# A gated GELU layer on one core: unit 1's weights loaded ahead of the transposed rows, and its raw products computed ahead of unit 0's second half

## The chip, the cores and the metric

The kernel runs on one core of a Trainium2 chip. The metric is the device time of one execution in microseconds. Times of two kernels are compared between runs of the same rounds on the same chip. All runs here were fast, with a granted TensorE clock of 0.999 to 1.0.

Names in the profile: PE is TensorE's matmuls and PEld its weight loads; DVE is VectorE, ACT ScalarE, POOL GpSimd; SPq is the queue that issues the DMA loads. A "bank" is one of the eight PSUM tiles of 128 x 512 float32 values in which TensorE leaves its products.

## The reference

```python
B, S, Dm, Df = 1, 2048, 1024, 3584           # all bfloat16
g = einsum("bsd,df->bsf", x, w_gate)
u = einsum("bsd,df->bsf", x, w_up)
h = gelu(g) * u                              # tanh form
return einsum("bsf,fd->bsd", h, w_down)
```

## The kernel before

The kernel goes through the rows of x in two passes of 1024 rows, each as two chunks of 512 columns of x transposed, `xT[0]` and `xT[1]`. In a pass it goes through 14 "units", each of 256 columns of `w_gate` and `w_up`. A unit is made by a Strassen-like scheme: seven products in place of eight, with sums of weight blocks (`s1` to `s4`, `sa`) and of x blocks (`t1` to `t4`, `tb`) made by VectorE, ScalarE and GpSimd. "Raw" products take w and xT as they are. Later stages do the same for `w_down`.

The change touches the opening only. Unit 0 of the first pass is done plainly (`plain`), chunk by chunk, because the sums are not ready yet. Unit 1 is the first by the scheme. Engines run what is listed for them in program order, except where a wait holds them.

```python
# the sums of one unit's weights (sh is 128 x 512)
"s1": lambda q: [new(eng, a21[i], a22[i], ADD, "s1", sh) for i in GU],
"s2": lambda q: [new(eng, q["s1"][i], a11[i], SUB, "s2", sh) for i in GU],
"s3": lambda q, GU=GU: [new(eng, a11[i], a21[i], SUB, "s3", sh) for i in GU],
"s4": lambda q: [new(eng, a12[i], q["s2"][i], SUB, "s4", sh) for i in GU],
"sa": lambda q: [cast(a22[i], "sa", sh) for i in GU],        # ScalarE
# ... and of x: t1 = lo1 - lo0, t2 = hi1 - t1, t3 = hi1 - lo1, t4 = hi0 - t2 (VectorE), tb = cast(hi1)

def unit(u, banks, xT, w, s, t, p1, after_p5, aside, keep, ahead_of_p4, snap_first):
    e, c, d = banks                      # for unit 1: banks 0-1, 2-3, 4-5
    for i in GU: product(c[i], w[:, i, KH:, :P], b21, True)      # raw
    aside(-2)
    g, up = add(c, p1)                   # two VectorE sums
    aside(-1)
    for i in GU: product(e[i], s["s2"][i], t["t2"], False)
    aside(0)
    # ... (copies of e; then c = d, banks 4 and 5)
    for i in GU: product(c[i], s["s1"][i], t["t1"], True)
    # ...
    for i in GU: product(e[i], s["s3"][i], t["t3"], False)
    # ...
    for i in GU: product(c[i], s["s4"][i], t["tb"], False)
    # ... (then the next unit's first raw product, then sa x t4)

# the loads of the opening, all on one queue
xn0 = load_x(0)                                     # 512 plain rows, transposed on PE
for k0, k1 in ((0, 2), (2, 5), (5, NKB)):
    load_wf(nc.sync, k0, k1)                        # unit 0's weights
for ko in range(KH):
    transposing(xT, 1, ko, N)                       # rows 512-1023, blocks 0-3, transposing DMA
w = load_w(1)                                       # unit 1's weights, 1 MB
for ko in range(KH, NKB):
    transposing(xT, 1, ko, N)                       # blocks 4-7
ahead = load_w(2)

# the work of the opening
plain(bank[0:4], 0, range(0, 2), parts=2)           # unit 0, first half of the rows
plain(bank[0:4], 0, range(2, NKB))
t.make("t1")
finish(bank[0:4], 0)                                # gelu on ScalarE, hT = g * bank on VectorE
plain(bank[4:8], 1, range(KH))                      # unit 0, second half, blocks 0-3
s.make("s1", "s2")
nxt = {"p1": first_product(odd, xT, w)}             # unit 1, raw

def rest_of_0(part):                                # called by unit 1's aside(-2), aside(-1)
    if part == 0:
        t.make("t2", "tb")
        plain(bank[4:8], 1, range(KH, NKB))         # blocks 4-7
        pool_behind(t["t2"][-1])                    # GpSimd waits for the last t2
        s["s3"] = on_pool(s, range(1))              # s3 on GpSimd
    else:
        t3 = t["how"]["t3"](t, range(0, 2))
        pool_behind(t3[-1])
        s["s3"] += on_pool(s, range(1, 2))
        finish(bank[4:8], 1)
        t["t3"] = t3 + t["how"]["t3"](t, range(2, KH))
        s.make("sa")
# and aside(0) makes s4, then t4
```

`finish` reads bank 5 in a VectorE multiply, and unit 1's `s1·t1` product writes bank 5 soon after. PE cannot start it before that multiply has ended.

Of the kernel before, what the change touches and what calls it, by code (L numbers as in the profile page):

```python
# [10 lines left out]
def kernel(  # L11
# [32 lines left out]
    ADD, SUB, MUL = ALU.add, ALU.subtract, ALU.mult  # L44
# [6 lines left out]
    NKB = Dm // P  # L51
    KH = NKB // 2
    NFB = Df // P
    NJ = NFB // 2
    N = 512
# [20 lines left out]
    def new_x():  # L76
        return [xpool.tile([P, NKB, N], bf16, name=f"xT{c}") for c in range(2)]
# [4 lines left out]
    def slot(shape, dtype, name):  # L82
        return kpool.tile(shape, dtype, name=name, tag="k")


    bank = [psum.tile([P, N], f32, name=f"bank{i}") for i in range(8)]
    even, odd, cc, dd = bank[6:8], bank[0:2], bank[2:4], bank[4:6]
# [7 lines left out]
    def new(eng, a, b, op, name, shape=None, dtype=None):  # L95
        t = slot(shape or [P, N], dtype or f32r, name)
        eng(t, a, b, op)
        return t

    def cast(src, name, shape=None):  # L100
        t = slot(shape or [P, N], f32r, name)
        nc.scalar.copy(out=t, in_=src)  # L102
        return t

    def snap(ps, name):
        t = slot([P, N], f32, name)
        nc.scalar.copy(out=t, in_=ps)  # L107
        return t

    def matmul(ps, lhs, rhs, start, stop):  # L110
        nc.tensor.matmul(  # L111
            ps, lhsT=lhs, rhs=rhs, start=start, stop=stop, skip_group_check=True
        )
# [35 lines left out]
    def sums_s(w, eng):  # L149
        GU = range(2)  # L150
        sh = [P, KH, P]
        a11, a21 = [[w[:, i, :KH, h : h + P] for i in GU] for h in (0, P)]
        a12, a22 = [[w[:, i, KH:, h : h + P] for i in GU] for h in (0, P)]
        return Sums(
            how={
                "s1": lambda q: [new(eng, a21[i], a22[i], ADD, "s1", sh) for i in GU],
                "s2": lambda q: [new(eng, q["s1"][i], a11[i], SUB, "s2", sh) for i in GU],
                "s3": lambda q, GU=GU: [new(eng, a11[i], a21[i], SUB, "s3", sh) for i in GU],
                "s4": lambda q: [new(eng, a12[i], q["s2"][i], SUB, "s4", sh) for i in GU],
                "sa": lambda q: [cast(a22[i], "sa", sh) for i in GU],  # L160
            }
        )

    def pool_behind(tile):
        nc.gpsimd.tensor_copy(out=seen, in_=tile[:, :1].bitcast(f32))
# [19 lines left out]
    def product(ps, lhs, rhs, start):  # L185
        for k in range(KH):
            matmul(ps, lhs[:, k, :], rhs[k], start and k == 0, k == KH - 1)

    def first_product(e, xT, w):
        for i in range(2):  # L190
            product(e[i], w[:, i, :KH, :P], [xT[0][:, k, :] for k in range(KH)], True)
        return [snap(e[i], "p1") for i in range(2)]
# [160 lines left out]
    sa = {}  # L353
# [97 lines left out]
    def transposing(xT, c, ko, r0):  # L451
        nc.sync.dma_start_transpose(
            out=xT[c][:, ko, :], in_=x2[r0 : r0 + N, ko * P : (ko + 1) * P]
        )
# [12 lines left out]
    xT = new_x()  # L467
    xn0 = load_x(0)
    wf = wpool.tile([P, 2, NKB, 2 * P], bf16, name="w")
    for k0, k1 in ((0, 2), (2, 5), (5, NKB)):  # L470
        load_wf(nc.sync, k0, k1)
    for ko in range(KH):
        transposing(xT, 1, ko, N)
    w = load_w(1)
    for ko in range(KH, NKB):
        transposing(xT, 1, ko, N)
    ahead = load_w(2)

    def plain(ps, c, kos, parts=1):
        n = N // parts  # L480
        for k in range(kos.start, kos.stop, 2):
            for part in range(parts):
                cols = slice(part * n, (part + 1) * n)
                for p, (j, i) in zip(ps, [(j, i) for j in range(2) for i in range(2)]):
                    for ko in (k, k + 1):
                        matmul(
                            p[:, cols],
                            wf[:, i, ko, j * P : (j + 1) * P],
                            xT[c][:, ko, cols],
                            ko == 0 and part == 0,  # L490
                            ko == NKB - 1,
                        )

    def finish(ps, c):
        for j in range(2):
            times(j, c, gelu(ps[2 * j]), ps[2 * j + 1])

    on_dve, on_act = nc.vector.tensor_copy, nc.scalar.copy
    s, t = sums_s(w, dve), sums_t(xT)
    with tc.manual_schedule(engines={ENG.Activation}):  # L500
        def keep_warm(n, cols):
            for _ in range(n):
                nc.tensor.matmul(  # L503
                    bank[3][:, :cols], lhsT=warm[:, :P], rhs=warm[:, :cols], start=True, stop=True
                )

        keep_warm(NWARM, N)
        for i in range(NS):
            if i > 0:
                keep_warm(3, 2 * P)  # L510
            turn(xT, xn0, 0, i, on_act if i == 1 else on_dve)
        plain(bank[0:4], 0, range(0, 2), parts=2)
        plain(bank[0:4], 0, range(2, NKB))
        t.make("t1")
        finish(bank[0:4], 0)
        plain(bank[4:8], 1, range(KH))
        s.make("s1", "s2")
        nxt = {"p1": first_product(odd, xT, w)}

    seen = xpool.tile([P, 1], f32, name="seen")  # L520
    on_pool = sums_s(w, pool)["how"]["s3"]

    def rest_of_0(part):
        if part == 0:
            t.make("t2", "tb")
            plain(bank[4:8], 1, range(KH, NKB))
            pool_behind(t["t2"][-1])
            s["s3"] = on_pool(s, range(1))
        else:
            t3 = t["how"]["t3"](t, range(0, 2))  # L530
            pool_behind(t3[-1])
            s["s3"] += on_pool(s, range(1, 2))
            finish(bank[4:8], 1)
            t["t3"] = t3 + t["how"]["t3"](t, range(2, KH))
            s.make("sa")

    def making(u):
        if u < 2 or u >= NU:
# [3 lines left out]
    for ip in range(NPASS):  # L542
        for u in range(1 if ip == 0 else 0, NU):
            js = making(u) if ip == 0 else []

            def prepare():
                nonlocal ahead
                if first:
                    pool_behind(t["t4"][-1])
                nxt["w"], nxt["s"] = ahead, None  # L550
                if u + 1 < NU:
                    nxt["s"] = make_s(ahead, pool)
                if u + 2 < NU:
                    ahead = load_w(u + 2)
                if len(js) == 1:
                    store_made(js[0])
                for j in js[1:]:
                    keep_whole(j)
                if ip == 0:
                    fetch_wd(making(u + 1))  # L560

            def keep(part, ps):
                if js:
                    keep_part(js[0], part, ps)

            def aside(part):
                if (ip, u) == (0, 1) and part < 0:
                    rest_of_0(part + 2)
                if part == 0 and "s4" not in s:
                    s.make("s4")  # L570
                    t.make("t4")

            def ahead_of_p4():
                if u + 1 < NU:
                    nxt["p1"] = first_product(even if u % 2 else odd, xT, nxt["w"])

            e = odd if u % 2 else even
            p1 = nxt.pop("p1", None) or first_product(e, xT, w)
            first = (ip, u) == (0, 1)
            with tc.manual_schedule(engines={ENG.Activation}) if first else nullcontext():  # L580
                unit(u, (e, cc, dd), xT, w, s, t, p1, prepare, aside, keep, ahead_of_p4, first)
            if u + 1 < NU:
                w, s = nxt["w"], nxt["s"]

        last = ip == NPASS - 1
        got, nxt = {}, {}

        def more(step):

            nonlocal ahead  # L590
            if last:
                return
            if step in (-1, 0, 2):
                store_made({-1: NJ - 3, 0: NJ - 2, 2: NJ - 1}[step])
            if step == 0:
                xT[:] = new_x()
            if step >= 24 and step % 2 == 0 and step // 2 - 12 < len(moves):
                c, ko = moves[step // 2 - 12]
                transposing(xT, c, ko, (2 * (ip + 1) + c) * N)
            if step == 50:  # L600
                got["w"], ahead = load_w(0), load_w(1)
            if step == 58:
                got["s"] = make_s(got["w"], dve)
            if step == 62:
                got["t"] = make_t(xT)

        down(ip, even + cc, dd + odd, last, more)
        even, odd, cc, dd = odd, even, dd, cc
        if not last:
            w, t, s = got["w"], got["t"], got["s"]  # L610
# [29 lines left out]
```

## Time and profile before

| | before |
|---|---|
| time, median of 3 runs (542.34 to 542.64) | 542.6 us |
| profiled span | 540.5 us |
| PE busy | 533.0 us, 99% |
| first product of unit 0 | 7.48 us |
| first `s2·t2` product of unit 1 | 24.73 us |
| first `s4·tb` product of unit 1 | 30.39 us |

Before the change, the page's row of busy times (us, share of the span, instructions) and its summary of the chain that ended last read as follows.

```profile
PE 533.0 (99%) x2380; PEld 378.3 (70%) x2414; DVE 340.8 (63%) x524; ACT 258.3 (48%) x463; POOL 238.9 (44%) x217
...
PE 98%; DMA 1%; issue 0%; SPq 0%; ACT 0%
```

PE is the engine that decides. A busy share of 99% alone would not prove that nothing is lost. The Trainium skill ("Trainium Kernel Development and Optimization", Performance Expectations) warns that matmul busy time is a bad metric for how close a kernel is to roofline, because matmuls are pipelined, and here weight loads are busy only 70%. So the count of matmuls is better. In PE's timeline (start, duration, engine, line, operation, out<-in, shape and count; idle time before in brackets), the opening looks like this:

```profile
7.48 17.61 PE L111 MATMUL bank<-xT,w 128*128 128x256 bf16 x86
24.73 5.82 PE L111 MATMUL bank<-t,s 128*128 128x512 f32 x24
30.39 1.97 PE L111 MATMUL bank<-tb,s 128*128 128x512 f32 x8
```

From 7.48 to 24.73 us PE does the work of 80 full-size bf16 matmuls, 0.216 us each. (The program has 88 here, 16 of them half-size; a few records are missing from the x86.) The following 24 take 5.66 us to the start of `tb`. No row has idle time in brackets.

VectorE's timeline in the same stretch does have idle time, and the DMA queue's timeline tells why:

```profile
11.06 1.92 DVE L90 TENSOR_TENSOR t<-xT,xT 128x512 fp32r<-128x512 bf16 x3 [2.69 <-DMA xT<-in_x_dram]
15.10 0.69 DVE L90 TENSOR_TENSOR t<-xT,xT 128x512 fp32r<-128x512 bf16 x1 [2.12 <-DMA xT<-in_x_dram]
15.71 1.28 DVE L90 TENSOR_TENSOR hT<-g,bank 128x512 bf16<-128x512 f32 x2
...
18.67 0.69 DVE L90 TENSOR_TENSOR s<-w 128x512 fp32r<-128x512 bf16 x1 [1.05 <-DMA w<-in_w_up_dram]
...
20.49 2.49 DVE L90 TENSOR_TENSOR t<-xT,t 128x512 fp32r<-128x512 bf16 x4
...
24.09 1.40 DVE L90 TENSOR_TENSOR t<-xT 128x512 fp32r<-128x512 bf16 x2
25.41 1.27 DVE L90 TENSOR_TENSOR hT<-g,bank 128x512 bf16<-128x512 f32 x2
26.61 1.47 DVE L90 TENSOR_TENSOR t<-xT 128x512 fp32r<-128x512 bf16 x2
```

```profile
6.22 5.47 SPq L452 DMA_TRANSPOSE xT<-in_x_dram  x4
11.73 0.58 SPq L121 DMA_DIRECT2D w<-in_w_gate_dram  x1
12.36 0.58 SPq L121 DMA_DIRECT2D w<-in_w_up_dram  x1
12.98 6.71 SPq L452 DMA_TRANSPOSE xT<-in_x_dram  x4
```

VectorE loses 2.69 + 2.12 + 1.05 us waiting for loads, but PE does not notice. The operand `t2` ends at 22.98 us and PE wants it from 24.73. The second pair of hT multiplies (25.41) frees bank 5 at about 26.1 us, and PE gets to bank 5 at about 24.73 + 12 x 0.236 = 27.6 us. The last `t3` ends at 28.1 us, and PE wants it at 24.73 + 19 x 0.236 = 29.2 us.

### The profile page before, as it was taken

How to read it: one execution, taken by the hardware profiler on the slowest of the kernel's cores; microseconds unless marked ns; L12 is line 12 of the kernel's file. 1: busy time of each engine (PE TensorE's matmuls, PEld its weight loads, DVE VectorE, ACT ScalarE, POOL GpSimd, SP SyncE). 2: the span in 40 equal slices, each digit the busy share in tenths (PEclk: the TensorE clock that was granted, in tenths of full speed). 3: DMA queues.
4: the chain of work that ended last, by engine and by line, in shares of the span. 5: the costliest groups of instructions: out<-in, count | busy, mean ns of one | idle time of the engine just before them, and what ended most of it. 6: DMA issues, size and time to landing. Idle time of an engine off the chain costs nothing.

```text
span 540.5 us, 7403 instructions
## 1 busy us (share of the span) xinstructions
PE 533.0 (99%) x2380; PEld 378.3 (70%) x2414; DVE 340.8 (63%) x524; ACT 258.3 (48%) x463; POOL 238.9 (44%) x217
## 2 busy tenths in 40 slices
PE   8999999999999999999999999999999999999997
PEld 5577777667766746888876776677777775488885
DVE  3896666766666895684945545555544559676730
ACT  2566666566665410255355555555555541114431
POOL 0169966677774400000097777777766600000000
PEclk9999999999999999999999999999999999999999
DMA  8965666666655899969672222222331069473751
GB/s 198 201 185 177 175 183 203 191 183 200 201 165 172 269 382 329 285 180 301 224 194 79 78 79 78 79 79 79 85 100 49 2 200 369 150 235 96 227 192 49
DMA packets 108133, 93.28 MB, mean 173 GB/s; under 512 B 17216, under 2 KB 92992, under 8 KB 108096
## 3 DMA queue, kind: packets, MB, share of 16 engines
q1 hardware_dynamic: 108096, 92.82, 58.8%
q8 instruction: 19, 0.31, 0.3%
q14 instruction: 18, 0.15, 0.1%
HBM read 74.45 MB, written 15.20 MB: 166 GB/s over the span
## 4 chain that ended last, share of the span: by engine, by line
PE 98%; DMA 1%; issue 0%; SPq 0%; ACT 0%
PE bank L111 98%; DMA xn<-in_x_dram 1%; PE bank L448 0%; SPq L441 0%; ACT st L412 0%; PE bank L503 0%
## 5 line engine op out<-in xcount | busy, mean ns | idle before, releaser
L93 POOL TENSOR_TENSOR s<-w 128x512 fp32r<-128x512 bf16 x102 | 119.4, 1191 | 154.7 <-DVE t L90 87.6
L111 PE MATMUL bank<-t,s 128*128 128x512 f32 x648 | 157.0, 398 | 0.0
L111 PEld LDWEIGHTS bank<-t,s 128*128 128x128 f32 x648 | 121.7, 188 | 27.7
L107 ACT COPY p<-bank 128x512 f32<-128x512 f32 x124 | 70.4, 591 | 97.4 <-PE bank L111 97.4
L111 PE MATMUL bank<-xT,w 128*128 128x512 bf16 (+1 forms) x476 | 110.6, 376 | 1.9
L90 DVE TENSOR_TENSOR hT<-g,bank 128x512 bf16<-128x512 f32 x112 | 76.6, 686 | 53.2 <-ACT g L179 47.7
L111 PEld LDWEIGHTS <-w 128*128 128x128 bf16 x504 | 45.1, 98 | 59.1 <-issue 13.4
L90 DVE TENSOR_TENSOR sum<-bank,p 128x512 f32<-128x512 f32 x54 | 37.3, 692 | 53.0 <-PE bank L111 51.3
L179 ACT ACTIVATE g<-sum 128x512 f32<-128x512 f32 x81 | 51.4, 635 | 34.1 <-DVE sum L90 33.1
L111 PE MATMUL bank<-q 128*128 128x512 f32 x240 | 58.9, 389 | 0.0
L111 PE MATMUL bank<-t,sa 128*128 128x512 f32 x216 | 58.6, 413 | 0.0
L93 POOL TENSOR_TENSOR s<-w,s 128x512 fp32r<-128x512 bf16 x50 | 57.6, 1172 | 0.0
L93 POOL TENSOR_TENSOR s<-s,w 128x512 fp32r<-128x512 f32 x50 | 57.1, 1164 | 0.0
L111 PE MATMUL bank<-tb,s 128*128 128x512 f32 x216 | 53.3, 389 | 0.0
L111 PEld LDWEIGHTS bank<-q 128*128 128x128 f32 x240 | 45.0, 188 | 9.3
L111 PE MATMUL bank<-raw,hT 128*128 128x512 bf16 x218 | 48.4, 379 | 0.3
L111 PEld LDWEIGHTS bank<-t,sa 128*128 128x128 f32 x216 | 40.7, 188 | 10.6
L111 PEld LDWEIGHTS bank<-tb,s 128*128 128x128 f32 x216 | 40.5, 188 | 8.4
L102 ACT CAST tb<-raw 128x512 fp32r<-128x512 bf16 x28 | 17.2, 626 | 59.8 <-DMA raw<-in_w_down_dram 26.3
L107 ACT COPY u<-bank 128x512 f32<-128x512 f32 x62 | 35.9, 590 | 18.6 <-PE bank L111 18.6
L90 DVE TENSOR_TENSOR bank<-bank,p 128x512 f32<-128x512 f32 x54 | 37.8, 699 | 8.5 <-PE bank L111 5.2
L90 DVE TENSOR_TENSOR q<-hT 128x512 fp32r<-128x512 bf16 x56 | 38.4, 686 | 4.8 <-PE bank L111 4.8
(45 smaller groups left out, 442.6 us busy)
## 6 DMA issues: line engine op xcount, KB each, us to landing
raw<-in_w_down_dram SPq DMA_DIRECT2D x80, 256.0 KB, 4.7
q<-td SPq DMA_DIRECT2D x60, 256.0 KB, 4.9
w<-in_w_gate_dram SPq DMA_DIRECT2D x27, 512.0 KB, 5.2
w<-in_w_up_dram SPq DMA_DIRECT2D x27, 512.0 KB, 6.3
td<-m SPq DMA_DIRECT2D x12, 768.0 KB, 4.6
w<-td SPq DMA_DIRECT2D x6, 1024.0 KB, 10.1
out_dram<-st SPq DMA_DIRECT2D x32, 128.0 KB, 1.7
td<-w SPq DMA_DIRECT2D x2, 768.0 KB, 7.0
```

The lines of the kernel that those rows point to most:

```text
L90: nc.vector.tensor_tensor(out=out, in0=a, in1=b, op=op)
L93: nc.gpsimd.tensor_tensor(out=out, in0=a, in1=b, op=op)
L102: nc.scalar.copy(out=t, in_=src)
L107: nc.scalar.copy(out=t, in_=ps)
L111: nc.tensor.matmul(ps, lhsT=lhs, rhs=rhs, start=start, stop=stop, skip_group_check=True)
L179: nc.scalar.activation(g, src, ACT.Gelu_apprx_tanh)
```

## The change

What the edit does: plain loads are issued in one run and transposing loads in one run, and the work is ordered to fit. Unit 1's weights come first, so its raw products, which need only `xT[0]`, go ahead of all of unit 0's second half, which needs the late `xT[1]`. The sums of weights come ahead of the sums of x, and `s3` no longer needs GpSimd.

```diff
 # loads
-    for ko in range(KH):
-        transposing(xT, 1, ko, N)
     w = load_w(1)
-    for ko in range(KH, NKB):
+    for ko in range(NKB):
         transposing(xT, 1, ko, N)
 # work
         plain(bank[0:4], 0, range(2, NKB))
+        s["s1"] = s["how"]["s1"](s, range(1))
+        finish(bank[0:4], 0)
+        s["s1"] += s["how"]["s1"](s, range(1, 2))
+        nxt = {"p1": first_product(odd, xT, w)}
+        s.make("sa", "s2", "s3", "s4")
         t.make("t1")
-        finish(bank[0:4], 0)
-        plain(bank[4:8], 1, range(KH))
-        s.make("s1", "s2")
-        nxt = {"p1": first_product(odd, xT, w)}
 # rest_of_0
         if part == 0:
+            plain(bank[4:8], 1, range(NKB))
             t.make("t2", "tb")
-            plain(bank[4:8], 1, range(KH, NKB))
-            pool_behind(t["t2"][-1])
-            s["s3"] = on_pool(s, range(1))
         else:
             t3 = t["how"]["t3"](t, range(0, 2))
-            pool_behind(t3[-1])
-            s["s3"] += on_pool(s, range(1, 2))
             finish(bank[4:8], 1)
             t["t3"] = t3 + t["how"]["t3"](t, range(2, KH))
-            s.make("sa")
 # aside(0): s4 is no longer made here, only t4  (cut: the GU argument moves from s3 to s1,
 # and the line that defines on_pool goes)
```

More of the change, by code (lines that the diff above doesn't have):

```diff
@@ L155, in sums_s @@
             how={
-                "s1": lambda q: [new(eng, a21[i], a22[i], ADD, "s1", sh) for i in GU],
+                "s1": lambda q, GU=GU: [new(eng, a21[i], a22[i], ADD, "s1", sh) for i in GU],
                 "s2": lambda q: [new(eng, q["s1"][i], a11[i], SUB, "s2", sh) for i in GU],
-                "s3": lambda q, GU=GU: [new(eng, a11[i], a21[i], SUB, "s3", sh) for i in GU],
+                "s3": lambda q: [new(eng, a11[i], a21[i], SUB, "s3", sh) for i in GU],
                 "s4": lambda q: [new(eng, a12[i], q["s2"][i], SUB, "s4", sh) for i in GU],
@@ L513 @@
         plain(bank[0:4], 0, range(2, NKB))
+        s["s1"] = s["how"]["s1"](s, range(1))
[3 more added lines that the diff above has]
+        s.make("sa", "s2", "s3", "s4")
         t.make("t1")
-        finish(bank[0:4], 0)
-        plain(bank[4:8], 1, range(KH))
-        s.make("s1", "s2")
-        nxt = {"p1": first_product(odd, xT, w)}
     seen = xpool.tile([P, 1], f32, name="seen")
-    on_pool = sums_s(w, pool)["how"]["s3"]
     def rest_of_0(part):
         if part == 0:
+            plain(bank[4:8], 1, range(NKB))
             t.make("t2", "tb")
-            plain(bank[4:8], 1, range(KH, NKB))
-            pool_behind(t["t2"][-1])
-            s["s3"] = on_pool(s, range(1))
         else:
             t3 = t["how"]["t3"](t, range(0, 2))
-            pool_behind(t3[-1])
-            s["s3"] += on_pool(s, range(1, 2))
             finish(bank[4:8], 1)
             t["t3"] = t3 + t["how"]["t3"](t, range(2, KH))
-            s.make("sa")
     def making(u):
@@ L568, in aside @@
                     rest_of_0(part + 2)
-                if part == 0 and "s4" not in s:
-                    s.make("s4")
+                if part == 0 and "t4" not in t:
                     t.make("t4")
```

## The prediction

> **What bounds the kernel now.** TensorE. The page's busy row gives PE 533.0 of 540.5 us (99%); the chain that ended last is 98% matmuls, DMA 1%. PE waits for x rows and their transposes until 7.5 us. In the timeline the opening's products run from 7.48 to 24.73 us: 80 full-size matmuls in 17.25 us, 0.216 us each, and the only wait listed there is 0.26 us for weights. So there is no hole of a microsecond to win; the change can save almost nothing on PE and can only open a new hole.
>
> **What the change moves.** No matmul is added or removed. On PE, the 16 raw products of unit 1 (3.4 us) go ahead of all 32 of unit 0's second half (6.8 us). On the queue, unit 1's weights go ahead of all eight transposing loads. In the before trace they are issued at 11.73 and land at 18.67 us, and VectorE waits three times: 2.7 + 2.1 us for transposed rows, 1.1 us for weights. After, the weights should land near 11.5 and 13 us (1 MB behind the first weights at the 290 GB/s of the DMA view), transposed rows by about 20 us, ahead of PE's need (17.8 to 23 us). These waits go, but VectorE's work is reordered: all s sums first, t1 and t2 last, and the two s3 sums move from GpSimd (1.17 us each) to VectorE (0.62 us cadence, +1.2 us).
>
> **What that costs.** VectorE starts in earnest only when the first gelus end (13.47 and 14.33 us + 0.6). From the second hT multiply at 14.95 us: it, s1, 2 s2, 2 s3, 2 s4, 4 t1, 4 t2 are 16 operations at 0.615 us, so t2 ends at 24.9 us instead of 22.98. Two sums, two t3, then the multiply that frees the fourth unit-0 bank: it ends at 27.9 us instead of 26.1. PE reaches that bank (second half of s1·t1) at 24.73 + 12 x 0.236 = 27.6 us and waits about 0.4 us. The last t3 comes at 29.8 us; PE wants it at 29.7: another 0.1 to 0.2 us. The t2 operands just arrive in time. Total +0.6 us, never recovered, since later units are back to back on PE (12.60 us each). GpSimd has unit 2's s2 ready near 37.0, PE wants it near 37.9: no further wait.
>
> The Trainium skill ("SBUF — State Buffer", engine-port section) says that a GpSimd operation and a VectorE one with two SBUF inputs lock each other out. One t3 of before took 0.869 us against 0.68 beside GpSimd's s3; this goes, worth 0.2 us of VectorE at most.
>
> **Prediction:** 543.2 us, range 542.3 to 544.4. Faster by over 2%: 0.003; within 2%: 0.99; slower by over 2%: 0.007.
>
> **What would show it.** PE's s/t stage still starts at 24.6 to 24.8 us; little or no VectorE wait for transposed rows; VectorE gapless from 15 to 32 us; a PE wait of 0.3 to 0.6 us near 27.6 us on the hT multiply, a smaller one on t3; the tb product starts near 31.0 instead of 30.39 us; then a constant shift to the end.
>
> **What would make it wrong.** Weights landing after 14 us (each microsecond adds one to PE's wait). Transposes slower in one run of eight, so that t1 or PE wait: up to +2 us. VectorE faster without GpSimd: then the waits vanish, 542.5. A gain over 0.3 us would mean a hidden PE loss in the opening.

## The result

| | before | changed |
|---|---|---|
| time, median of 6 runs | 542.38 us (542.08 to 542.64) | 542.78 us (542.38 to 543.27) |
| ratio of fast runs | | 1.0008, 95% interval 0.9995 to 1.0021 |
| profiled span | 540.5 us | 540.6 us |

A ratio is the mean time of one kernel's fast runs over that of the other's of the same rounds, so it is not quite the ratio of the medians. The timing alone does not tell whether the change costs 0.4 us or nothing. The trace does.

After the change, the page's rows for PE and the chain:

```profile
PE 535.9 (99%) x2414; PEld 378.8 (70%) x2414; DVE 341.4 (63%) x526; ACT 258.7 (48%) x463; POOL 236.4 (44%) x213
...
PE 99%; ACT 0%; DVE 0%; issue 0%
```

(PE's 2.9 us more of busy time is 34 more matmul records: 2414 against 2380. The program has the same matmuls, as the 2414 weight loads in both rows show; a later trace of the changed kernel, `a_after`, has 2380 records and 533.4 us. So PE's busy time must not be compared between traces with different numbers of records.) PE's timeline after:

```profile
7.18 17.52 PE L111 MATMUL bank<-xT,w 128*128 128x256 bf16 x88
24.35 6.22 PE L111 MATMUL bank<-t,s 128*128 128x512 f32 x24
30.41 1.99 PE L111 MATMUL bank<-tb,s 128*128 128x512 f32 x8
```

The opening started 0.30 us earlier in this trace and the first `s·t` product 0.38 us earlier, yet `tb` starts at the same time. The block of 24 products from the first `s2·t2` to the first `s4·tb` grew from 5.66 to 6.06 us. The timelines of weight loads say where. Before, the 24 loads are one row without a wait:

```profile
24.71 5.42 PEld L111 LDWEIGHTS bank<-t,s 128*128 128x128 f32 x24
```

After:

```profile
24.32 2.72 PEld L111 LDWEIGHTS bank<-t,s 128*128 128x128 f32 x12
27.34 1.46 PEld L111 LDWEIGHTS bank<-t,s 128*128 128x128 f32 x7 [0.31 <-DVE hT L90]
29.15 0.99 PEld L111 LDWEIGHTS bank<-t,s 128*128 128x128 f32 x5 [0.35 <-DVE t L90]
```

After 12 loads (`s2·t2` for both halves, `s1·t1` for the first) PE waits for VectorE's hT multiply: that is bank 5. After 19 it waits for `t3`, the last block. VectorE's timeline after:

```profile
12.00 0.69 DVE L90 TENSOR_TENSOR s<-w 128x512 fp32r<-128x512 bf16 x1 [3.92 <-DMA w<-in_w_gate_dram]
13.71 0.69 DVE L90 TENSOR_TENSOR hT<-g,bank 128x512 bf16<-128x512 f32 x1 [1.02 <-ACT g L179]
14.57 0.69 DVE L90 TENSOR_TENSOR hT<-g,bank 128x512 bf16<-128x512 f32 x1 [0.18 <-ACT g L179]
...
21.80 2.49 DVE L90 TENSOR_TENSOR t<-xT,t 128x512 fp32r<-128x512 bf16 x4
...
25.41 1.29 DVE L90 TENSOR_TENSOR t<-xT 128x512 fp32r<-128x512 bf16 x2
26.61 1.28 DVE L90 TENSOR_TENSOR hT<-g,bank 128x512 bf16<-128x512 f32 x2
27.80 1.29 DVE L90 TENSOR_TENSOR t<-xT 128x512 fp32r<-128x512 bf16 x2
```

The waits for transposed rows are gone from VectorE, and from 14.57 us it has no gap. But the same operations come later: `t2` ends at 24.29 us (22.98 before), the bank-freeing multiply starts at 26.61 (25.41 before), the last `t3` ends at 29.1 (28.1 before). VectorE was ahead of PE; now it is behind by a few tenths.

The queue's timeline after, and ScalarE's casts of the last four transposed blocks, show how late those rows come:

```profile
5.76 0.74 SPq L121 DMA_DIRECT2D w<-in_w_gate_dram  x1
6.55 2.00 SPq L121 DMA_DIRECT2D w<-in_w_up_dram  x1
8.59 12.66 SPq L452 DMA_TRANSPOSE xT<-in_x_dram  x8
```

```profile
19.67 1.21 ACT L102 CAST tb<-xT 128x512 fp32r<-128x512 bf16 x2 [1.94 <-DMA xT<-in_x_dram]
21.68 0.62 ACT L102 CAST tb<-xT 128x512 fp32r<-128x512 bf16 x1 [0.81 <-DMA xT<-in_x_dram]
22.84 0.62 ACT L102 CAST tb<-xT 128x512 fp32r<-128x512 bf16 x1 [0.54 <-DMA xT<-in_x_dram]
```

Unit 1's first weights are there at 12.00 us; the last transposed block only at 22.84 us. In this trace that costs PE nothing.

### The profile page after: what moved, and what is told of

Same layout as the page of the kernel before. It is cut to its first block, busy times and chain, and to the rows that moved or that the text cites. A ratio compares the mean times of both kernels' runs of the same rounds, so it can differ in the third digit from the quotient of the medians.

```text
span 540.6 us, 7439 instructions
## 1 busy us (share of the span) xinstructions
PE 535.9 (99%) x2414; PEld 378.8 (70%) x2414; DVE 341.4 (63%) x526; ACT 258.7 (48%) x463; POOL 236.4 (44%) x213
## 4 chain that ended last, share of the span: by engine, by line
PE 99%; ACT 0%; DVE 0%; issue 0%
PE bank L111 98%; PE bank L501 1%; PE bank L448 0%; ACT st L412 0%; DVE warm L432 0%
## 5 line engine op out<-in xcount | busy, mean ns | idle before, releaser
L93 POOL TENSOR_TENSOR s<-w 128x512 fp32r<-128x512 bf16 x100 | 116.9, 1189 | 154.9 <-PE bank L111 154.9
L111 PE MATMUL bank<-xT,w 128*128 128x512 bf16 (+1 forms) x504 | 116.2, 377 | 0.0
```

What stands on the lines that cost most here:

```text
L93: nc.gpsimd.tensor_tensor(out=out, in0=a, in1=b, op=op)
L111: nc.tensor.matmul(ps, lhsT=lhs, rhs=rhs, start=start, stop=stop, skip_group_check=True)
```

## The experiments

The theory (A): the changed order leaves VectorE's chain of single operations, which begins with the first gelus, without slack. PE loses 0.40 us in the block of 24 products, and nothing else of the change has a cost or a gain. Rival B: the earlier start of the opening belongs to the new order of loads and is a real gain that offsets the loss. Rival C: all of it is noise.

Since the runs start at slightly different times, two differences are read from each trace: the block (first `s2·t2` to first `s4·tb` product) and the stretch from unit 0's first product to the first `s4·tb` product. The rest of the kernel, from that product to the end of the span, was 510.1 to 510.3 us in every trace but one (`two_more`, 510.5).

| kernel | first product, us | block, us | first product to `tb`, us | ratio to before (95%) |
|---|---|---|---|---|
| before | 7.48 | 5.66 | 22.91 | |
| n_before | 7.85 | 5.68 | 22.85 | 1.0 (0.9986 to 1.0013) |
| changed | 7.18 | 6.06 | 23.23 | 1.0008 (0.9995 to 1.0021) |
| a_after | 7.43 | 6.06 | 23.33 | 1.0015 (1.0003 to 1.0028) |
| a_after_2 | 8.26 | 6.06 | 23.23 | 1.0008 (0.9994 to 1.0021) |
| s3_on_pool | 6.84 | 5.65 | 22.90 | 1.0005 (0.9992 to 1.0017) |
| s4_late | 7.10 | 5.67 | 22.89 | 0.9997 (0.9984 to 1.0009) |
| s3_pool_s4_late | 7.89 | 5.66 | 22.82 | 1.0001 (0.9988 to 1.0013) |
| free_bank_first | 7.89 | 6.07 | 23.32 | 1.0005 (0.9992 to 1.0017) |
| two_more | 6.80 | 7.26 | 24.43 | 1.0023 (1.0011 to 1.0036) |
| loads_only | 7.33 | 5.65 | 24.36 | 1.0022 (1.0006 to 1.0037) |
| order_only | 6.97 | 5.96 | 25.38 | 1.0035 (1.0022 to 1.0049) |

All outputs are right. The intervals of the times are as wide as the effect (0.001 is 0.54 us), so for the small effects the trace columns carry the verdict and the times only have to agree. They do within their intervals.

### The null run and two repeats

No edit: the kernel before again, and the changed kernel twice more.

> The kernel before, unchanged, as a null run. Theory A (VectorE's chain costs the changed kernel 0.40 us on PE between the start of the s/t products and the start of the tb products; the 0.38 us by which the changed kernel's s/t products started earlier is chance of the first loads): time within 0.15 us of before, block from s/t start to tb start 5.66 us, start of the first product anywhere from 7.1 to 7.6 us. Rival B (the earlier start belongs to the new load order): first product again near 7.48 us and s/t start near 24.73 us.

> The changed kernel, unchanged, again. Theory A: +0.3 to +0.5 us against before; block from s/t start to tb start 6.0 to 6.1 us with the two waits (hT multiply, t3) of about 0.3 us; start of the first product scattered as in the kernel before. Rival B: start again near 7.18 us, s/t start near 24.35 us, and no difference in time. Rival C (noise only): interval well inside plus or minus 0.2 us and centred on zero.

> The changed kernel once more, for a third timing against before and a third trace. Theory A: +0.3 to +0.8 us against before, block 6.06 us, from first product to tb start 23.2 to 23.35 us; start of the first product anywhere between 6.8 and 7.9 us.

The block repeats to 0.02 us: 5.66 and 5.68 before, 6.06 three times changed. The start does not repeat. In the two traces of before it is 7.48 and 7.85 us, in the three of the changed kernel 7.18, 7.43 and 8.26. With the experiments, the new order of loads has nine traces from 6.80 to 8.26 us (mean 7.41), the old order three from 6.97 to 7.85 (mean 7.43). Rival B (a start near 7.48 before and near 7.18 changed, each time) is refuted. Traces that scatter by 1.5 us cannot exclude a shift of a few tenths, but if there were such a gain, the three relieved kernels below, with the new loads and a block of about 5.66 us, would be faster than before, and their times show no sign of it (1.0005, 0.9997, 1.0001). Nor is the scatter all due to the first loads, which both kernels issue alike: in eight traces the first product follows the landing of its first weights by 0.1 to 0.3 us, in four (`n_before`, `a_after_2`, `s3_pool_s4_late`, `loads_only`) by 1.2 to 1.6 us. In `a_after_2` the third group of eight transposing matmuls, just before, took 0.99 us, in the changed kernel's first trace 0.61 us; why was not tested. Three expectations missed: the null run started later than the 7.6 us allowed for, `a_after_2` later than 7.9, and `a_after`'s time was 0.81 us above before where 0.3 to 0.5 was expected. The three timings of the changed kernel are all above before, by 0.08%, 0.15% and 0.08%; the middle one is clear of one. Rival C (all noise) falls with the block above all; the three times agree with it.

### s3_on_pool: the two s3 sums back on GpSimd

```diff
         s["s1"] = s["how"]["s1"](s, range(1))
+        s["s3"] = sums_s(w, pool)["how"]["s3"](s)
         finish(bank[0:4], 0)
 ...
-        s.make("sa", "s2", "s3", "s4")
+        s.make("sa", "s2", "s4")
```

> The changed kernel with the two s3 sums back on GpSimd (as in before, but at once when the weights land, behind no VectorE operation). Takes 1.2 us from VectorE's chain. Theory A: both PE waits vanish, block 5.66 us again, time 0.4 us below the changed kernel, equal to before within 0.15 us. t2 can gain less than 1.2 us since the last transposed row lands at 22.8 us, which keeps t2's end at 23.5 us or later. If the loads or the order of the raw products were the cause: block stays near 6.06 us.

Both waits vanished, and the block is back at 5.65 us. The caution about late rows was not needed: `t2` ended at 22.83 us, the last row having been there by 21.72 in this trace, whose opening started early. The time, 1.0005, lies between the two kernels, with one run of five at 543.0 us, and cannot decide.

### s4_late: the two s4 sums put back behind t3

```diff
-        s.make("sa", "s2", "s3", "s4")
+        s.make("sa", "s2", "s3")
 ...
                 if part == 0 and "t4" not in t:
+                    s.make("s4")
                     t.make("t4")
```

> The changed kernel with the two s4 sums put back behind t3, where before has them. Takes the same 1.2 us from ahead of the hT multiply and t3 without touching GpSimd. Theory A: both PE waits vanish, block 5.66 us, time 0.4 us below the changed kernel. If instead GpSimd's absence or presence mattered (rival: two engines locking each other out), this differs from the run with s3 on GpSimd by 0.2 us or more.

PE's timeline of this run:

```profile
7.10 17.57 PE L111 MATMUL bank<-xT,w 128*128 128x256 bf16 x86
24.32 5.83 PE L111 MATMUL bank<-t,s 128*128 128x512 f32 x24
29.99 1.98 PE L111 MATMUL bank<-tb,s 128*128 128x512 f32 x8
```

The start of 24.32 is that of the changed kernel (24.35), but `tb` comes at 29.99 in place of 30.41 us. GpSimd does nothing different here, and the block differs from that of `s3_on_pool` by only 0.02 us. So what counts is VectorE's time ahead of the hT multiply, not which engine makes the sums. The time (541.84 us, against 542.81 for the changed kernel in the same rounds) agrees with a loss undone, and is not clear of before's 542.01.

### s3_pool_s4_late: both reliefs together

The edits of the two runs above, both.

> The changed kernel with both reliefs: s3 on GpSimd and s4 behind t3, 2.4 us less on VectorE ahead of the hT multiply. Theory A: one relief of 1.2 us already took both waits away, so the second is worth nothing: block 5.66 us, time within 0.2 us of before, 0.4 to 0.7 us below the changed kernel of the same rounds. If PE still had a hidden loss in the opening: faster than before by 0.3 us or more, and from first product to tb start less than 22.85 us.

The block is 5.66 us and the whole stretch 22.82, 0.03 us below the null run. One relief of 1.2 us had already removed both waits, and the second buys nothing: VectorE's chain causes no other loss of PE there.

### free_bank_first: the hT multiplies ahead of all four t3 sums

```diff
-            t3 = t["how"]["t3"](t, range(0, 2))
             finish(bank[4:8], 1)
-            t["t3"] = t3 + t["how"]["t3"](t, range(2, KH))
+            t["t3"] = t["how"]["t3"](t)
```

> The changed kernel with the two hT multiplies that free unit 0's banks put ahead of all four t3 sums, instead of between them. The bank comes free 1.2 us earlier; the last t3 comes at the same time. Theory A1 (the two waits stand one behind the other on one VectorE chain and the last t3 alone decides): the wait for hT vanishes, the wait for t3 grows to 0.5 us or more, block from s/t start to tb start stays 6.0 to 6.1 us, time as the changed kernel's, +0.4 us. Rival A2 (the waits add up): block near 5.85 us, time +0.2 us.

The timeline of weight loads of this run:

```profile
25.12 4.07 PEld L111 LDWEIGHTS bank<-t,s 128*128 128x128 f32 x18
29.34 0.19 PEld L111 LDWEIGHTS bank<-t,s 128*128 128x128 f32 x1 [0.15 <-DVE t L90]
29.94 1.00 PEld L111 LDWEIGHTS bank<-t,s 128*128 128x128 f32 x5 [0.42 <-DVE t L90]
```

The wait for the bank is gone, the waits for `t3` add up to 0.57 us, and the block is 6.07 us as in the changed kernel. So the two waits stand one behind the other on one chain, and its last member alone sets the loss (A1). Removing the wait that comes first in the list is worth nothing.

### two_more: 1.2 us more on VectorE

```diff
         s.make("sa", "s2", "s3", "s4")
+        for i in range(2):
+            dve(s["s3"][i], w[:, i, :KH, :P], w[:, i, :KH, P:], SUB)   # same values again
```

> The changed kernel with the two s3 sums made twice (same values) on VectorE, so two more operations, 1.2 us, ahead of t1. Theory A: no slack is left on VectorE's chain, so PE loses all of it: block 7.2 to 7.3 us instead of 6.06, time +1.2 us against the changed kernel, +1.6 us against before. Rival (chain not binding, the 0.4 us come from elsewhere): less than +0.5 us.

PE's timeline:

```profile
23.97 3.54 PE L111 MATMUL bank<-t,s 128*128 128x512 f32 x12
28.17 3.23 PE L111 MATMUL bank<-t,s 128*128 128x512 f32 x12 [0.66 <-DVE hT L90]
31.23 1.99 PE L111 MATMUL bank<-tb,s 128*128 128x512 f32 x8
```

The block is 7.26 us, exactly 1.20 more than changed: PE lost all of the time that was added to VectorE's chain. The time, +0.23% or about 1.25 us against before, is somewhat under the 1.6 expected, with 1.6 inside its interval.

### loads_only and order_only: each half of the change alone

`loads_only` is the kernel before with the changed block of loads; `order_only` is the changed kernel with the block of loads of before (both blocks as in the diff above).

> The order of loads of the changed kernel with the order of work of before. The first four transposed blocks then land near 14, 15.3, 16.5 and 17.7 us (worked back from the waits for the last four in the changed kernel), where PE wants them from 14.5 us. PE waits for them and for the banks behind t1: s/t products start 1.7 us later (1.0 to 2.5), time +1.5 to +2 us. If the order of loads alone were harmless or good, as a rival would have it: within 0.3 us of before.

> The order of work of the changed kernel with the order of loads of before. Unit 1's weights land at 16.4 and 18.0 to 18.7 us, and PE wants them at 14.4 and 15.2 us: it waits about 2 us and then 1 more, and VectorE's chain starts 3.4 us later. s/t start near 27.5 to 28 us, block again about 6.1 us or more, time +3.5 to +4 us against before.

PE's timeline of the first and of the second:

```profile
7.33 9.10 PE L111 MATMUL bank<-xT,w 128*128 128x256 bf16 x48
17.81 8.58 PE L111 MATMUL bank<-xT,w 128*128 128x512 bf16 x38 [1.39 <-DMA xT<-in_x_dram]
26.04 5.82 PE L111 MATMUL bank<-t,s 128*128 128x512 f32 x24
```

```profile
6.97 7.19 PE L111 MATMUL bank<-xT,w 128*128 128x256 bf16 x39
15.34 1.04 PE L111 MATMUL bank<-xT,w 128*128 128x512 bf16 x4 [1.18 <-DMA w<-in_w_gate_dram]
17.07 9.67 PE L111 MATMUL bank<-xT,w 128*128 128x512 bf16 x43 [0.69 <-DMA w<-in_w_up_dram]
```

With the new loads and the old work, PE waits 1.39 us for transposed rows at 17.81 us, and the stretch is 1.5 us longer than the null run's; the time is about 1.2 us longer, less than the 1.5 to 2 expected, with an interval up to 2.0. With the old loads and the new work it waits 1.18 and 0.69 us for weights, and the stretch is 2.5 us longer. The two halves belong together: each order of work fits its own order of loads. The size of the second was missed: +3.5 to +4 us was expected and 2.5 (trace) or about 1.9 (time) came. The landing times had been taken from traces with a later start; here the weights were there at 15.3 and 17.1 us, not 16.4 and 18.0 to 18.7. Its block, 5.96 us, is also a little under the 6.1 expected.

## Why the prediction was right

- **"No hole of a microsecond to win; the change can only open a new hole."** Held. Both reliefs together give a stretch of 22.82 us where before has 22.85 and 22.91.
- **"VectorE's waits go, but VectorE's work is reordered; t2 ends at 24.9 us."** Held: 24.29 us in a trace that starts 0.30 us earlier, and 24.64 in `a_after`, whose first product at 7.43 us is nearly that of the trace that was predicted from. The weights, forecast for about 11.5 and 13 us, landed at 11.98 and 13.67.
- **"The multiply that frees the fourth bank ends at 27.9 us, PE wants it at 27.6."** Held in kind: in `a_after` VectorE's multiply starts at 26.96 and so ends at about 27.6 us, and PE waits. `two_more` shows that the chain binds (1.20 us more of it cost PE 1.20 us), `s3_on_pool` and `s4_late` that relieving it undoes the loss.
- **"Total +0.6 us."** Mis-sized. The two waits on the weight loads are 0.31 + 0.35 = 0.66 us, yet the block grew by 0.40. The Trainium skill ("TensorE: Matmul & The Clock Gate", Architectural detail) says that PE's queue can pull weight loads ahead of matmuls in flight. The trace agrees: in the changed kernel's records a load ordinarily starts about 0.22 us before its own matmul, but the load after the first wait only 0.002 us before. So a wait of a load first uses up this lead, and the starts of the matmuls around the two waits are late by only about 0.15 us (bank) and 0.19 us (`t3`); the rest of the 0.40 is slightly wider spacing elsewhere. No run varied the lead by itself. The term that was mis-sized is thus the bank's wait, put at 0.4 and measured at about 0.15; the one for `t3`, put at 0.1 to 0.2, was right. The chain behind both was reckoned too long: VectorE's operations came every 0.602 us in `a_after`, not 0.615, so the bank's multiply ended about 0.26 us earlier and the last `t3` (29.44 us, forecast 29.8) 0.36 us earlier than reckoned. The `tb` product came at 30.41 and 30.76 us, not near 31.0.
- **"Transposed rows by about 20 us."** Wrong in size, without effect: the last came at 22.84 us (22.25 in `a_after`), when PE first read it at 23.0 us (23.4 in `a_after`) and VectorE's last `t2` at 23.6. The margin that had looked like 3 us was 0.2 us (1.1 in `a_after`). The eight issues took 12.66 us: six took about 1.26 us each, the median of before, but the first and the fifth 2.4.
- **"GpSimd beside VectorE costs VectorE 0.2 us at most."** The skill's page ("SBUF — State Buffer", SBUF: two separate sides) has the two engines exclude each other where VectorE reads two SBUF inputs while GpSimd reads SBUF too, as s3 does. The traces agree with a small effect on VectorE: the first pair of `t3` sums took 1.40 us beside GpSimd's s3 in before and in the null run, 1.29 in the changed kernel without it. They also show the other side: in `s3_on_pool` GpSimd's first s3, started just after a VectorE s1 of two SBUF inputs, took 1.65 us, its second, beside an hT multiply that has one input in PSUM, 1.16 us.
- **"Then a constant shift to the end."** Held: 510.1 us from the `tb` product to the end before, 510.2 after.

The measured +0.4 us (0.43, 0.81 and 0.43 by the ratios of the three timings, times 542) lies inside the range given, at two thirds of the predicted shift. By itself the time proves little: its interval runs from 0.3 us faster to 1.1 us slower, and that the medians differ by just the 0.40 us of the block is partly luck. What bears the prediction out is the two waits in the trace, where it had put them. What was also unforeseen is the scatter of the start, 1.5 us between traces, which is larger than the effect.

No version beat both kernels. The changed kernel with one relief equals the one before.

## What to carry to other kernels

When the engine that decides has no gap, look at how far ahead of it the helpers are at each hand-over; a change that clears a helper's waits can still move its last result behind the moment of need, and then the helper's delay becomes a loss. Look at the last member of such a chain, not at the first wait in the list: moving the bank's release forward here bought nothing, and taking 1.2 us out of the chain, in either of two ways, bought back the whole 0.40 us. For effects below the scatter of the time, measure a stretch between two events in the trace, and repeat the unchanged kernel.

## What the Trainium skill lacked or had wrong

- "Advanced Engine Details and Errata", X-Bar Transpose (TRN2), says that transpose DMAs are as fast as regular DMAs, 350 to 400 GB/s. Here eight transposing loads of 128 KB each, issued in a row on one queue, did not reach that as a series: they took 12.66 us to issue, and the last two landed 1.15 us apart, which is about 114 GB/s. That does not refute the page's figure for the transfer: the first three landed only 0.47 and 0.44 us apart, and in `a_after` the DMA rate of the last blocks comes in bursts of up to 250 GB/s with lulls near zero between them. This points to the issues, about 1.3 us apart; no run varied them.
- No page that I found gives the issue time on the queue of one transposing load of this size (512 x 128 elements): 1.26 us median in the opening of before and up to 2.8 us, against 0.58 us for a plain load of unit 1's weights.
- "TensorE: Matmul & The Clock Gate" has the weight loads run ahead, but not what it does to the reading of a wait: 0.66 us of waits on weight loads came with 0.40 us of lost PE time.
- No page that I found mentions how much the start of a kernel scatters: unit 0's first product came between 6.80 and 8.26 us in twelve traces whose first loads are issued alike.
